# The preparation stage of a gated attention and S4 training kernel: parameter arithmetic on VectorE, gate sums as a row of a key projection, four staging tiles, later constant rows, value stores from GpSimd's queue

## Chip, cores and metric

The kernel runs on one core of a Trainium2 chip, as one launch. The metric is the device time of that launch in microseconds (us). The times given are medians over runs; the profile is of one execution.

## What is computed

The kernel computes the output of a gated mixture of two branches on the same input x (2048 positions, 576 features), and the gradients of everything but the second branch's own input. Cut to what matters:

```python
g = sigmoid((x * gate_w).sum(-1, keepdims=True))          # one gate per position
q, k, v = split_heads(x @ wqkv)                           # 32 heads of width 18
a = softmax(q @ k.T * 18**-0.5) @ v @ wo                  # branch A: attention

dt = exp(log_dt)[:, None]                                 # branch B: S4, 576 channels x 128 states
P  = exp(dt * (A_re + 1j*A_im) * l)                       # l = 0 .. 2047
K  = einsum("dn,dnl,dn->dl", C, P, dt * B).real
b  = causal_convolution(K, x) + x * Dskip
out = g * a + (1 - g) * b
# returned: out, and the gradients for x, wqkv, wo, A_re, A_im, B_re, B_im, C_re, C_im, log_dt, Dskip, gate_w
```

## The kernel before

The kernel has three stages that follow one another: preparation (lines 128 to 447), attention forward and backward in one loop (811 to 1263), then the S4 branch and the final products (1265 on). The change touches the preparation alone. In all three the order of instructions on each engine is the order in which the program issues them (a manual schedule, line 129): an engine that waits holds back all that is behind it on the same engine, and the DMA queue of SyncE (SP), which is written in the same way, does so too. Up to eight transfers issued from SP and ACT share a ring of eight completion semaphores, so a transfer also waits for the one that last used its semaphore.

Preparation, in the order of the program:

- Loads (182 to 198), all from SP: x in four blocks of four tiles of 128 positions, the K, Q and V columns of wqkv (`load_w`), gate_w broadcast to all partitions, the six S4 parameters (`load_prm`, three buffers `blk3` in turn), log_dt, then the constant rows of `QKV_d` (195 to 196, from a small DRAM tile `cst_d`) and wo.
- `x_turn` (213) transposes a block of x on TensorE into `xT`; `x_rev` (225) multiplies each tile by a reversal matrix, copies it to a staging tile `xr_t` (tag "xr", two buffers) and stores the staged block to DRAM (`xr_d`, line 234). Blocks 0 and 1 go ahead of the loop, 2 and 3 at its step 1.
- A loop of 30 steps (434 to 446). A step is one head group m (7 heads, the last 4), one of K, Q, V (`which` 1, 0, 2) and one half of the positions. It runs `proj` (347: ten matmuls of 512 columns into a PSUM tile of two buffers), `norms` of the step two before (363: two matmuls into one PSUM tile; for K a VectorE maximum `kmx`, for Q a ScalarE square root `qn`), `take` (384: the PSUM tile is copied to `stg`, by ScalarE, for the second half of V by VectorE, and squared on VectorE into `sq` for K and Q), and then the step's jobs. At the second half `stg` is stored to `QKV_d`: K and Q from ACT's queue, V from SP's (line 399; in the first group from SP as well).
- Jobs (409 to 426) are small pieces hung on steps: `prm_turn` (245, transposes of the parameters, steps 2 to 7), `gate_sum` (236: VectorE multiplies a tile of x by `gate_r` and sums each row, sixteen times, steps 0 to 10), `gate_fin` (239, step 11), `pars(k)` (297, steps 8 to 13: the S4 parameters, mostly on GpSimd through the helper `pl`, line 295; the results go to DRAM in `par_d`, `dt_d`, `prm_d` from GpSimd's queue), `wo_turn` (251, steps 12 to 16), `load_go` and `scale_go` (259 and 263: two loads of grad_out at step 7, and its products with g and 1 - g on VectorE at steps 14, 15, 20, 23, each of the first two followed by another load; the second product uses the tag "xr" too), and `da_turn` (274, steps 17 to 28).

Attention begins by loading strips of `QKV_d` from SP: `KaT_g` (line 854), `QaT_g` (865), and `Vtok_g` by a DMA transpose (869). Its tiles lie in memory that the preparation's pool has given back, so each waits for the last reader of what lay there. The first ScalarE work there is the exponential of line 1234. GpSimd begins with two memsets (841), loads `ez` from `par_d` (477) and then computes the S4 basis in the background (470, 523), and per block of queries `dOa` (908), which VectorE and TensorE wait for.

Of the kernel before, what the change touches and what calls it, by code (L numbers as in the profile page):

```python
# [20 lines left out]
def build(tc, aps, dbg_aps=None, stages=("s1", "attn", "post", "s4", "final")):  # L21
# [40 lines left out]
    with ExitStack() as gctx:  # L62
# [65 lines left out]
        with ExitStack() as ctx:  # L128
# [14 lines left out]

            xb = [s1.tile([P, TB, D], BF, name=f"xb{tb}") for tb in range(NBK)]
            blk3 = [s1.tile([P, DC, N], BF, name=f"pblk{q}") for q in range(3)]
            gate_r = s1.tile([P, D], BF, name="gate_r")
            gj = s1.tile([P, D], BF, name="gj")
            tmpb = s1.tile([P, D], BF, name="rowb")
            w_sb = s1.tile([P, DC, F], BF, name="wqkv_sb")
            xT = s1.tile([P, DC, S], BF, name="xT")  # L150
            wo_sb = s1.tile([P, DC, DPAD], BF, name="wo_sb")
            prm = s1.tile([P, 6, D], BF, name="prm")
            con = s1.tile([P, 3, S // P], BF, name="con")
            hsel = s1.tile([P, P], BF, name="hsel")
            gsum = s1.tile([P, NT], F32, name="gsum")
# [3 lines left out]
            for q_, v_ in enumerate((0.0, -1.0, 1.0)):  # L159
                GP.memset(con[:, q_, :], v_)  # L160
            GP.memset(hsel, 1.0)
# [7 lines left out]
            def load_w(which):  # L169
                sl = slice(which * D, (which + 1) * D)  # L170
                nc.sync.dma_start(w_sb[:, 0:nf, sl], wqkv[0:nf * P, sl].rearrange("(c p) n -> p c n", p=P))
                for y in range(2):
                    nc.sync.dma_start(w_sb[y * HB:(y + 1) * HB, nf, sl], wqkv[nf * P:D, sl])
# [7 lines left out]

            load_x(0, 0, 2)
# [6 lines left out]
            nc.sync.dma_start(gate_r, gate_w.rearrange("(o d) -> o d", o=1).to_broadcast([P, D]))  # L189
            load_prm(0)  # L190
            load_prm(1)
            load_w(2)
            nc.sync.dma_start(tmpb, log_dt.rearrange("(o d) -> o d", o=1).to_broadcast([P, D]))
            load_prm(2)
            for q_, (y0, y1) in enumerate(((DH + 1, HP), (DH, HS), (DH, HS))):
                nc.sync.dma_start(rows[q_][:, y0:y1, :], cst_d[q_:q_ + 1].unsqueeze(1).to_broadcast([H, y1 - y0, S]))
            nc.sync.dma_start(wo_sb[:, 0:nf, 0:D], wo[0:nf * P, :].rearrange("(c p) n -> p c n", p=P))
            nc.sync.dma_start(wo_sb[0:HB, nf, 0:D], wo[nf * P:D, :])
# [26 lines left out]
            def x_rev(t, eng):  # L225
                tb, q = divmod(t, TB)
                if q == 0:
                    xr_t[tb] = s1.tile([P, TB, D], BF, tag="xr", bufs=2, name="xr_t")
                ps = psJ.tile([P, 2, 512], F32, tag="pj", name="psr")
                for u in range(2):  # L230
                    mm(ps[:, u, 0:DH2], lhsT=J_bf, rhs=xb[tb][:, q, u * DH2:(u + 1) * DH2])
                copy_of(eng)(xr_t[tb][:, q, :].rearrange("p (u f) -> p u f", u=2), ps[:, :, 0:DH2])
                if q == TB - 1:
                    nc.sync.dma_start(xr_d[:, tb * TB:(tb + 1) * TB, :], xr_t[tb])

            def gate_sum(t):
                V.scalar_tensor_tensor(gj, xb[t // TB][:, t % TB, :], 1.0, gate_r, op0=A.mult, op1=A.mult, accum_out=gsum[:, t:t + 1])
# [7 lines left out]
            def prm_turn(r_, eng):  # L245
                b_ = blk3[r_ % 3]
                turn_rows([(b_[:, c, :], P, P) for c in range(nf)] + [(b_[0:HB, nf, :], HB, P)], None, eng, prm[:, r_, :])
# [9 lines left out]
            gob, dab = {}, {}  # L257

            def load_go(b):
                gob[b] = s1.tile([P, TB, D], BF, tag="go", bufs=2, name="go_b")  # L260
                nc.sync.dma_start(gob[b], go_v[:, b * TB:(b + 1) * TB, :])

            def scale_go(b):
                dab[b] = s1.tile([P, TB, D], BF, tag="d_a", bufs=2, name="d_a")
                gy_b = s1.tile([P, TB, D], BF, tag="xr", bufs=2, name="gy_b")
                for q in range(TB):
                    t = b * TB + q
                    V.tensor_scalar(dab[b][:, q, :], gob[b][:, q, :], g_t[:, t:t + 1], None, op0=A.mult)
                    V.tensor_scalar(gy_b[:, TB - 1 - q, :], gob[b][:, q, :], omg_t[:, t:t + 1], None, op0=A.mult)
                nc.sync.dma_start(gyr_d[:, NT - (b + 1) * TB:NT - b * TB, :], gy_b)  # L270
                if b + 2 < NBK:
                    load_go(b + 2)
# [12 lines left out]
            dt_b = s1.tile([P, D], F32, name="dt_b")  # L285
            adt = s1.tile([P, D], F32, name="adt")
            thn = s1.tile([P, D], F32, name="thn")
            t1 = s1.tile([P, D], F32, name="t1")
            Wn = s1.tile([P, 4, D], F32, name="Wn")
            wz = s1.tile([P, 2, D], F32, name="wz")  # L290
            zt = [s1.tile([P, 4, D], F32, name=f"zt{q}") for q in range(2)]
            POW = (1, P)

            def pl(o, a, b, op):
                GP.tensor_tensor(o, a, b, op=op)

            def pars(k):
                Ar_n, Ai_n, Br_n, Bi_n, Cr_n, Ci_n = [prm[:, r_, :] for r_ in range(6)]
                Wr, Wi = Wn[:, 0, :], Wn[:, 1, :]
                if k == 0:  # L300
                    AC.activation(dt_b, tmpb, ACT.Exp)
                    pl(adt, Ar_n, dt_b, A.mult)
                    pl(thn, Ai_n, dt_b, A.mult)
                elif k == 1:
                    for z_, p_ in zip(zt, POW):
                        AC.activation(z_[:, 0, :], adt, ACT.Exp, scale=float(p_))
                    for z_, p_ in zip(zt, POW):
                        V.tensor_scalar(z_[:, 2, :], thn, float(p_) * INV2PI, None, op0=A.mult)
                        V.tensor_scalar(z_[:, 1, :], z_[:, 2, :], MAGIC, -MAGIC, op0=A.add, op1=A.add)
                        V.tensor_tensor(z_[:, 2, :], z_[:, 2, :], z_[:, 1, :], op=A.subtract)  # L310
                elif k == 2:
                    pl(Wr, Cr_n, Br_n, A.mult); pl(t1, Ci_n, Bi_n, A.mult)
                    pl(Wr, Wr, t1, A.subtract); pl(Wr, Wr, dt_b, A.mult)
                    pl(Wi, Cr_n, Bi_n, A.mult); pl(t1, Ci_n, Br_n, A.mult)
                    pl(Wi, Wi, t1, A.add); pl(Wi, Wi, dt_b, A.mult)
                    GP.tensor_scalar(Wn[:, 2:4, :], Wn[:, 0:2, :], -1.0, None, op0=A.mult)
# [3 lines left out]
                elif k == 3:  # L320
                    for z_ in zt:
                        AC.activation(z_[:, 1, :], z_[:, 2, :], ACT.Sin, scale=0.5 * TWO_PI)
                        AC.activation(z_[:, 3, :], z_[:, 2, :], ACT.Sin, scale=0.25 * TWO_PI)
                else:
                    z_ = zt[k - 4]
                    gm, c_, s_, q_ = [z_[:, y, :] for y in range(4)]
                    pl(q_, q_, q_, A.mult)
                    GP.tensor_scalar(q_, q_, -4.0, 2.0, op0=A.mult, op1=A.add)
                    pl(s_, c_, q_, A.mult)
                    pl(c_, c_, c_, A.mult)  # L330
                    GP.tensor_scalar(c_, c_, -2.0, 1.0, op0=A.mult, op1=A.add)
                    pl(c_, gm, c_, A.mult)
                    pl(s_, gm, s_, A.mult)
                    if k == 4:
                        GP.dma_start(par_d[:, 8:10, :], z_[:, 1:3, :])
                        pl(wz[:, 0, :], Wr, c_, A.mult); pl(t1, Wi, s_, A.mult); pl(wz[:, 0, :], wz[:, 0, :], t1, A.subtract)
                        pl(wz[:, 1, :], Wr, s_, A.mult); pl(t1, Wi, c_, A.mult); pl(wz[:, 1, :], wz[:, 1, :], t1, A.add)
                        GP.dma_start(par_d[:, 4:6, :], wz)
                    else:
                        GP.tensor_scalar(q_, s_, -1.0, None, op0=A.mult)  # L340
                        GP.dma_start(par_d[:, 1:4, :], z_[:, 1:4, :])
                        GP.dma_start(par_d[:, 0:1, :], z_[:, 1:2, :])

            steps = [(m, which, pr) for m in range(len(hts)) for which in (1, 0, 2) for pr in range(2)]
            stgs, sqs = {}, {}

            def proj(s):
# [4 lines left out]
                w0 = which * D + h0 * DH  # L352
# [31 lines left out]
            def take(s, ps):  # L384
# [8 lines left out]
                on_v = which == 2 and pr == 1  # L393
                if which == 0:
# [3 lines left out]
                if pr == 1:  # L398
                    (nc.sync if on_v and s > 2 else AC).dma_start(rows[which][h0:h0 + hn, 0:DH, :], stg[0:fn, :])
# [9 lines left out]
            for r_, (s, e) in enumerate(((2, V), (3, V), (4, AC), (5, AC), (6, AC), (7, AC))):  # L409
                job(s, lambda r_=r_, e=e: prm_turn(r_, e))  # L410
            for k, s in enumerate((8, 9, 10, 11, 12, 13)):
                job(s, lambda k=k: pars(k))
            t = 0
# [1260 lines left out]
```

## Time and profile before

| what | us |
|---|---|
| median of 3 runs (2786.41 to 2802.28) | 2798.0 |
| profiled execution, its own time | 2800.34 |
| its span in the profile | 2798.6 |
| TensorE busy in the span | 2432.4 |
| VectorE busy | 2367.5 |
| ScalarE busy | 2367.9 |
| GpSimd busy | 1653.1 |
| first 160 us: TensorE / VectorE / ScalarE / GpSimd busy | 104.2 / 100.2 / 67.1 / 56.7 |
| first matmul of the attention stage starts at | 170.93 |

The profile is one execution; its span is 1.7 us shorter than the time of that execution, and that execution is 2.3 us above the median. Times in the views count from the start of the span. PE is TensorE, DVE VectorE, ACT ScalarE, POOL GpSimd, SP SyncE; "SPq" is SP's DMA queue issuing. L232 is line 232 of the kernel; a helper's line stands for all its callers.

### The profile page before, as it was taken

The page shows a single profiled execution, that of the slowest core. Times are in us where ns is not written, and L with a number is a line of the kernel's source. Part 1 is how long each engine was busy: PE and PEld are TensorE (multiplying, and loading weights), DVE is VectorE, ACT ScalarE, POOL GpSimd, SP SyncE. Part 2 cuts the span into 40 slices and gives each one's busy share as a digit, 9 for nine tenths or more (in the row PEclk, how much of TensorE's full clock was granted, in tenths as well). Part 3 has the DMA queues.
Part 4 walks back from the last instruction along what each step waited for, and adds up shares of the span by engine and source line. Part 5 has one row for each costly group of instructions (what it writes and reads, how often), then busy time and mean ns, then how long its engine had stood idle before and what let it go on. Part 6 is the DMA issues. An engine that isn't in the chain of part 4 may idle for free.

```text
span 2798.6 us, 70648 instructions
## 1 busy us (share of the span) xinstructions
PE 2432.4 (87%) x27379; PEld 1166.5 (42%) x27379; DVE 2367.5 (85%) x4862; ACT 2367.9 (85%) x2749; POOL 1653.1 (59%) x2694
## 2 busy tenths in 40 slices
PE   6678989989898889989989998898885899988789
PEld 3332333333233333333333333333323888888557
DVE  4837999999888999989999999898885899999944
ACT  3459999999999999999999999999974788888221
POOL 0757887988888798888878879878701000000010
PEclk8888999999998999999999999999987898899899
DMA  6435889879988988998897898798669998986996
GB/s 201 158 93 129 158 157 181 159 163 170 164 157 148 181 165 158 176 172 151 165 177 157 160 180 156 160 167 166 153 131 214 243 248 215 246 239 173 252 238 136
DMA packets 1253515, 490.95 MB, mean 175 GB/s; under 512 B 1150005, under 2 KB 1224486, under 8 KB 1243962
## 3 DMA queue, kind: packets, MB, share of 16 engines
q1 hardware_dynamic: 1218282, 416.29, 72.8%
q0 software_dynamic: 21536, 57.40, 8.0%
q10 hardware_dynamic: 13360, 12.75, 1.6%
q8 instruction: 214, 3.51, 0.5%
q14 instruction: 123, 1.01, 0.1%
HBM read 145.83 MB, written 98.52 MB: 87 GB/s over the span
## 4 chain that ended last, share of the span: by engine, by line
ACT 36%; PE 24%; DVE 24%; issue 6%; DMA 5%; POOL 3%; SPq 1%; ACTq 0%; DVEq 0%; POOLq 0%
ACT eb L1239 21%; ACT PT L1234 13%; PE ps_P L30 7%; DVE ds L1244 7%; DVE tz L672 3%; PE accV L30 2%; DVE tz L674 2%; PE turn_p L956 2%; DVE HG L676 2%; PE ps_dx L30 2%; PE ps_proj L30 2%; DVE pq L742 1%; PE accK L30 1%; POOL et L470 1%; DVE dvacc L1010 1%
## 5 line engine op out<-in xcount | busy, mean ns | idle before, releaser
L1244 DVE TENSOR_TENSOR ds<-ps_P,PT 128x512 bf16<-128x512 f32 x2048 | 1310.9, 682 | 136.5 <-PE ps_P L30 89.5
L1239 ACT ACTIVATE eb<-ps_P 128x1024 bf16<-128x1024 f32 x1024 | 1099.9, 1074 | 39.9 <-PE ps_P L30 39.9
L1234 ACT ACTIVATE PT<-ps_P 128x1024 bf16<-128x1024 f32 x1024 | 1105.2, 1080 | 24.0 <-PE ps_P L30 22.5
L30 PE MATMUL ps_P<-dOaT,VaT_g 32*128 32x512 bf16 x2048 | 579.9, 391 | 30.0 <-DVE ds L1244 15.4
L470 POOL TENSOR_TENSOR et<-eG,eT 128x448 f32<-128x448 f32 x576 | 542.2, 961 | 10.7
L30 PE MATMUL ps_P<-QaT_g,KaT_g 32*128 32x512 bf16 x2048 | 405.7, 388 | 140.1 <-ACT PT L1234 122.7
L30 PE MATMUL ps_P<-KaT_g,QaT_g 32*128 32x512 bf16 x2048 | 409.5, 392 | 2.0 <-ACT eb L1239 1.5
L30 PEld LDWEIGHTS <-KaT_g 32*128 32x128 bf16 x2048 | 147.9, 91 | 467.2 <-issue 451.4
L470 POOL TENSOR_TENSOR Eo<-et,et 128x448 bf16<-128x448 f32 x288 | 326.9, 1135 | 20.8
L778 POOL TENSOR_TENSOR SS<-m 128x96 f32<-128x96 f32 x18 | 9.5, 528 | 428.7 <-ACT m L776 428.7
L30 PEld LDWEIGHTS <-QaT_g 32*128 32x128 bf16 x2048 | 116.2, 91 | 289.7 <-issue 267.5
L30 PE MATMUL accV<-eb,dOa 128*32 128x512 bf16 x2048 | 186.7, 398 | 27.6 <-ACT eb L1239 27.2
L30 PE MATMUL accO<-PT,Vtok_g 128*32 128x512 bf16 x2048 | 208.4, 396 | 0.1
L30 PE MATMUL accK<-dsT,Qtok_g 128*32 128x256 bf16 x4096 | 163.9, 281 | 15.9 <-DMA dsT<-ds 14.1
L30 PE MATMUL accQ<-ds,Ktok_g 128*32 128x512 bf16 x2048 | 162.5, 396 | 2.1 <-DVE dvacc L1010 2.0
L30 PEld LDWEIGHTS <-Vtok_g 128*32 128x32 bf16 x2048 | 52.8, 93 | 221.8 <-issue 221.8
L961 DVE COPY dsT<-turn_p 128x1024 bf16<-128x1024 bf16 (+1 forms) x216 | 138.8, 643 | 1.8 <-PE turn_p L956 1.7
L956 PE MATMUL turn_p<-ident_bf,ds 128*128 128x128 bf16 x1664 | 134.9, 224 | 2.1 <-DVE dkacc L1047 0.9
L633 ACT COPY E1e<-etp 128x1024 bf16<-128x1024 bf16 x136 | 128.9, 1063 | 4.3 <-PE etp L632 4.1
L672 DVE TENSOR_TENSOR tz<-HG,par 128x128 f32<-128x128 f32 x504 | 123.4, 284 | 0.6
L470 POOL TENSOR_TENSOR et<-eT 128x32 f32<-128x32 f32 (+3 forms) x288 | 115.8, 422 | 11.4
L30 PEld LDWEIGHTS <-Qtok_g 128*32 128x32 bf16 x4096 | 88.3, 97 | 80.4 <-issue 54.6
(257 smaller groups left out, 3737.7 us busy)
## 6 DMA issues: line engine op xcount, KB each, us to landing
E_d<-Eo POOLq DMA_DIRECT2D x144, 256.0 KB, 3.4
E1n<-E_d SPq DMA_DIRECT2D x36, 1024.0 KB
xs<-xb_d SPq DMA_DIRECT2D x18, 1024.0 KB
T0w<-Kp_d SPq DMA_DIRECT2D x18, 1024.0 KB
Md_d<-mst SPq DMA_DIRECT2D x36, 288.0 KB
dsT<-ds SPq DMA_TRANSPOSE x512
dqkv_d<-dtk POOLq DMA_DIRECT2D x96, 72.0 KB, 4.1
skw<-Md_d SPq DMA_DIRECT2D x72, 64.0 KB
```

The source lines that it names most:

```text
L30: return nc.tensor.matmul(out, lhsT=lhsT, rhs=rhs, start=start, stop=stop, **kw)
L470: nc.gpsimd.tensor_tensor(out, a, b, op=op)
L633: copy(E_[:, 4 * q:4 * q + 4], pt_)
L672: nc.vector.tensor_tensor(tz[s_], HG[:, s_, :, k - 1, :].unsqueeze(1).to_broadcast([P, 2, 2, CB]), ZZ, op=A.mult)
L674: nc.vector.tensor_tensor(tz[s_][:, 0], tz[s_][:, 0], UVk[:, :, s_, k, :], op=A.add)
L676: nc.vector.tensor_tensor(HG[:, s_, :, k, :], tz[s_][:, 0], tz[s_][:, 1, ::-1], op=A.add)
L742: nc.vector.tensor_tensor(o.rearrange("p a b n c -> p a b (n c)"), a_.rearrange("p b n c -> p b (n c)").unsqueeze(1).to_broadcast([P, 2, 2 ...
L956: nc.tensor.transpose(pt_[:, x, qb, :], t_[:, qb * P:(qb + 1) * P], ident_bf)
L961: (nc.scalar.copy if NTOT <= now[0] < NTOT + OFF else nc.vector.tensor_copy)(o_(), pt_[:, x:x + n])
L1234: nc.scalar.activation(U["PT"][i, j // 2], ps, ACT.Exp)
L1239: nc.scalar.activation(e, ps, ACT.Exp)
L1244: nc.vector.tensor_tensor(U["ds"][i][:, j, :], ps, U["PT"][i, j // 2][:, j % 2, :], op=A.mult)
```

## The change

All of it is in the preparation.

- Parameters: `pars` has eleven pieces instead of six, at steps 6, 7, 8, 9, 10, 11, 12, 16, 17, 22, 23. All arithmetic is on VectorE (`tt`) with both powers side by side in one operand of 1152 elements; exponentials and sines stay on ScalarE. GpSimd keeps the stores.
- Gate sums: gate_w is loaded as one more column of the weights, 24 zero columns behind the K columns (`GCOL`), so that the K projection of the last head group gives the sums as row 96 of its PSUM tile. ScalarE copies that row (`gate_take`), eight one-column matmuls turn it into columns (`gate_turn`). The last head group therefore runs second: m in the order 0, 4, 1, 2, 3. The sixteen `gate_sum` operations go.
- Staging: tag "xr" has four buffers. `d_a` takes these tiles afterwards; grad_out is loaded over the tiles of x, all four blocks at step 3, and its second product is written in place and stored tile by tile (16 stores in place of 4). `scale_go` comes in halves at steps 13 to 16 and 18 to 21.
- Loads: the gate column follows wq; parameters, log_dt and wv are issued after step 0 and so behind the first two `xr_d` stores; wo at step 2, constant rows at step 4. The turns of the last two parameters move to steps 8 and 9.
- V stores go out from GpSimd's queue.
- The order of allocation changes, so that the tiles of attention lie over other tiles of the preparation (`zt` is now the first).

```diff
+            WOFF = {1: 0, 0: 608, 2: 1184}
+            GCOL, GROW = D + 24, 96
+            zt = s1.tile([P, 4, 2, D], F32, name="zt")
+            w_sb = s1.tile([P, DC, 1760], BF, name="wqkv_sb")
...
+            V.memset(w_sb[:, :, D:GCOL], 0.0)
+            V.memset(one_f, 1.0)
...
+            def load_gate():
+                nc.sync.dma_start(w_sb[:, 0:nf, GCOL], gate_w[0:nf * P].rearrange("(c p) -> p c", p=P))
+                for y in range(2):
+                    nc.sync.dma_start(w_sb[y * HB:(y + 1) * HB, nf, GCOL:GCOL + 1], gate_w[nf * P:D].rearrange("(p o) -> p o", o=1))
...
-                    xr_t[tb] = s1.tile([P, TB, D], BF, tag="xr", bufs=2, name="xr_t")
+                    xr_t[tb] = s1.tile([P, TB, D], BF, tag="xr", bufs=4, name="xr_t")
...
-            def gate_sum(t):
-                V.scalar_tensor_tensor(gj, xb[t // TB][:, t % TB, :], 1.0, gate_r, op0=A.mult, op1=A.mult, accum_out=gsum[:, t:t + 1])
+            def gate_take(pr, ps):
+                zrow[pr] = s1.tile([P, 2 * TW], F32, tag="zrow", name="zrow")
+                AC.copy(zrow[pr][GROW:GROW + 1], ps[GROW:GROW + 1].rearrange("p a b -> p (a b)"))
+
+            def gate_turn(pr):
+                z_ = zrow.pop(pr)
+                pz = psT.tile([P, 512], F32, tag="tr", name="pz")
+                nb = 2 * TB
+                for q in range(nb):
+                    mm(pz[:, q:q + 1], lhsT=z_[GROW:GROW + 1, q * P:(q + 1) * P], rhs=one_f[GROW:GROW + 1, :], tile_position=(GROW, 0))
+                V.tensor_copy(gsum[:, pr * nb:(pr + 1) * nb], pz[:, 0:nb])
...
+                for q in range(q0, q0 + 2):
                     t = b * TB + q
-                    V.tensor_scalar(dab[b][:, q, :], gob[b][:, q, :], g_t[:, t:t + 1], None, op0=A.mult)
-                    V.tensor_scalar(gy_b[:, TB - 1 - q, :], gob[b][:, q, :], omg_t[:, t:t + 1], None, op0=A.mult)
-                nc.sync.dma_start(gyr_d[:, NT - (b + 1) * TB:NT - b * TB, :], gy_b)
+                    V.tensor_scalar(dab[b][:, q, :], xb[b][:, q, :], g_t[:, t:t + 1], None, op0=A.mult)
+                    V.tensor_scalar(xb[b][:, q, :], xb[b][:, q, :], omg_t[:, t:t + 1], None, op0=A.mult)
+                    nc.sync.dma_start(gyr_d[:, NT - 1 - t, :], xb[b][:, q, :])
...
+                elif k == 4:
+                    tt(Wn[:, 2:4, :], prm[:, 4:6, :], prm[:, 2:4, :], A.mult)
+                    tt(tp, prm[:, 4:6, :], prm[:, 3:1:-1, :], A.mult)
+                    tt(Wn[:, 0, :], Wn[:, 2, :], Wn[:, 3, :], A.subtract)
+                elif k == 5:
+                    tt(Wn[:, 1, :], tp[:, 0, :], tp[:, 1, :], A.add)
+                    tt(Wn[:, 0:2, :], Wn[:, 0:2, :], bc, A.mult)
+                    V.tensor_scalar(Wn[:, 2:4, :], Wn[:, 0:2, :], -1.0, None, op0=A.mult)
+                    GP.dma_start(par_d[:, 6:8, :], Wn[:, 2:4, :])
...
-            steps = [(m, which, pr) for m in range(len(hts)) for which in (1, 0, 2) for pr in range(2)]
+            steps = [(m, which, pr) for m in (0, 4, 1, 2, 3) for which in (1, 0, 2) for pr in range(2)]
+            GATE = (4, 1)
...
-                    (nc.sync if on_v and s > 2 else AC).dma_start(rows[which][h0:h0 + hn, 0:DH, :], stg[0:fn, :])
+                    (GP if on_v else AC).dma_start(rows[which][h0:h0 + hn, 0:DH, :], stg[0:fn, :])
...
-            for r_, (s, e) in enumerate(((2, V), (3, V), (4, AC), (5, AC), (6, AC), (7, AC))):
+            for r_, (s, e) in enumerate(((2, V), (3, V), (4, AC), (5, AC), (8, AC), (9, AC))):
...
-            for k, s in enumerate((8, 9, 10, 11, 12, 13)):
+            for k, s in enumerate((6, 7, 8, 9, 10, 11, 12, 16, 17, 22, 23)):
...
-            job(11, gate_fin)
-            job(7, lambda: [load_go(b) for b in range(2)])
+            job(12, gate_fin)
+            job(2, load_wo)
+            job(3, lambda: [load_go(b) for b in range(NBK)])
+            job(4, load_const)
...
+                if s == 0:
+                    late_tiles()
+                    load_prm(0)
+                    load_prm(1)
+                    nc.sync.dma_start(prm_t["tmpb"], log_dt.rearrange("(o d) -> o d", o=1).to_broadcast([P, D]))
+                    load_w(2)
+                    load_prm(2)
```

## Prediction

> **What bounds the kernel now.** I read the page first, then busy time by stretches of 10 us, then the waits, then the chain in order of time, all for the preparation.
>
> ```profile
> PE   6678989989898889989989998898885899988789
> DVE  4837999999888999989999999898885899999944
> ACT  3459999999999999999999999999974788888221
> ```
>
> Each digit is 70 us. The first two are low on all three engines, then ScalarE stands at 9 for most of the attention. What the preparation saves should therefore come off the end one for one: attention starts earlier and does not run faster. By stretches (us, then per engine busy time and count, granted clock, DMA):
>
> ```profile
> 20.00:30.00 10.00, 0.00 (x0) 0.00 (x0) 0.00 (x0) 0.00 (x0) 0.00 (x0) 0.61 0.96 234
> ...
> 80.00:90.00 10.00, 0.00 (x0) 0.00 (x0) 9.86 (x11) 2.58 (x4) 9.44 (x6) 0.51 0.00 0
> ...
> 100.00:110.00 10.00, 3.64 (x20) 1.88 (x20) 10.00 (x9) 1.02 (x1) 9.37 (x8) 0.87 0.44 148
> ...
> 160.00:170.00 10.00, 0.00 (x0) 0.00 (x0) 0.00 (x0) 0.00 (x0) 8.83 (x29) 0.50 0.74 112
> ```
>
> Four holes of TensorE: one with only DMA, two under VectorE and GpSimd busy together, one at the border to attention. The waits of the first 180 us name them (total, times, longest):
>
> ```profile
> PE psr L30 <- ACT xr_t L232: 19.5, 2, 18.8
> ACT xr_t L232 <- DMA xr_d<-xr_t: 19.1, 1, 19.1
> ...
> PE ps_P L30 <- DMA QaT_g<-QKV_d: 15.1, 1, 15.1
> ...
> PE ps_proj L30 <- DVE stg L397: 13.6, 2, 13.1
> ...
> PE ps L30 <- DVE kmx L373: 9.9, 2, 9.6
> ```
>
> The first hole is the third staging tile waiting for the first one's store, which SP issued only at 23.91 us, behind the constants and wo, and which landed at 36.5. The next two are PSUM tiles that VectorE frees late. Why VectorE is late shows by form of operation (count, busy, mean ns), first in the preparation, then late in the kernel where GpSimd is nearly idle:
>
> ```profile
> L310 DVE TENSOR_TENSOR zt<-zt 128x576 f32<-128x576 f32 x2 | 3.5, 1772 | 0.1
> ...
> L268 DVE TENSOR_SCALAR d_a<-go_b,g_t 128x576 bf16<-128x576 bf16 x16 | 13.6, 849 | 0.0
> ```
>
> ```profile
> L1393 DVE TENSOR_TENSOR fta<-zz,SS 128x576 f32<-128x576 f32 x6 | 4.5, 748 | 0.0
> ...
> L1497 DVE TENSOR_SCALAR Wri_f<-Wri_f 128x576 f32<-128x576 f32 x1 | 0.5, 453 | 0.0
> ```
>
> The same subtraction shape takes 1772 ns beside GpSimd and 748 without it; `d_a` takes 0.35 us where GpSimd rests and 1.5 where it works. The border, from the chain:
>
> ```profile
> 155.87 1.11 ACT qn L380
> 157.35 0.59 SPq L854
> ...
> 162.76 2.34 SPq L869
> 165.22 5.58 DMA QaT_g<-QKV_d
> ```
>
> The strips for attention are issued only after the last V store, since both are in SP's queue.
>
> [...] Here GpSimd's stores of 288 to 864 KB landed 3.1 to 8.4 us after issue. [...] The trace has the 1.28 (at 66.76), and the exponential follows at 68.06[...].
>
> **The change part by part.** Landmarks before: step 1 starts on TensorE at 43.3, step 6 at 58.0, the last `qn` at 155.9, the first exponential of attention at 171.6.
>
> *Four tiles, loads moved behind the stores.* Reversals of blocks 2 and 3 no longer wait for any store. Last work before the hole ends at 18.4, the wait ends at 36.5: 18.1 us go. The remaining reversal, 37.2 to 43.3, ran at half clock (0.50) and becomes about 5: in all -18.5 (17 to 20). Is something else late then? Step 1 needs wk, long there; wq for step 2 was complete by 16.5; wv, now behind the gate column and two stores, is needed at step 4, near 33, and its 0.65 MB should land by 26 at 250 GB/s. The gate column is 640 elements of 2 bytes; nothing to 5 us, taken 2, hidden, because SP's next items (`xr_d`, parameters, wv) have slack of that size.
>
> *Steps 1 to 5.* 14.7 us, bound by TensorE (2.7 to 3.1 a step, by what turns and norms stand in it). Unchanged.
>
> *Steps 6 to 29.* Before 97.9 us. I walked these steps with trace durations: projection 2.2, norms 0.45, a turn 0.5 to 0.65; ScalarE copy 1.0, `qn` 1.1; VectorE `sq` 0.67, `kmx` 1.21, V copy 1.22, scaling 0.36 each.
> - Parameters on VectorE: 12 two-operand operations of 1152 at 1.35 (between 748 for 576 and L691's 2159 for 1920), 4 of 576 at 0.75, single-operand ones at 0.75 and 0.45: 23 us. Off VectorE go gate sums (16.9 + 1.3), the old L308 to L310 (9.5), and the excess of scaling (24.7 to 11.5) and `sq` (3): 44. GpSimd is left with stores.
> - Gate: ScalarE row copies 2 x 1.0 (an operation of 1024 columns costs that whatever its rows), 16 one-column matmuls. None is shown; nearest are L898's float32 transposes, 0.165 each. I take 0.15, 2.4 us in all; bounds 0.1 to 0.3.
> - A new wait: the row tile has one buffer, and step 7's row copy stands on ScalarE ahead of step 7's `stg` copy while step 8's `gate_turn` still has to read the old row. So ScalarE waits through projection 8, norms, a turn and eight matmuls, about 2.5 us beyond its own work; projection 9 waits for the `stg` copy queued behind it, and `kmx`, `sq` and the sines follow late. Cost in the walk: 4 us.
> - Sums by six steps: steps 6 to 11 TensorE 18.1, VectorE 17.5, ScalarE 19.0, with the new wait 24; steps 12 to 17 TensorE 17.6, VectorE 22, now the bound; 18 to 23 TensorE 18.3, VectorE 19.3; 24 to 29 17.5, as measured (138.35 to 155.87). The walk overlaps neighbours and ends at 81.5.
> So -16.5 (10 to 21).
>
> *V stores and strips at the border.* SP now reaches the strips after its last `gyr_d` store (step 21); `KaT` waits for the last reader of `zt` (step 22), `QaT` for the semaphore of the K store of step 25. With some 3 us for that store and the 5.6 that `QaT` took, it lands about 3 us before the last step ends. Left are `qn` 1.1, table load 1.28, half a microsecond: 3 in place of 15.7, -12.7 (-14 to -8). Behind it the first five rounds ran 8.3 us at clock 0.54 where later ones take 6.3; a warm TensorE saves 0 to 2, taken 1. Of the V stores on GpSimd, each buffer is reused five steps, 15 us, later: covered by landing times up to 8.4. GpSimd starts its own work after the last V store, only some 36 us earlier against 49 for the rest; before its first `dOa` it had idled 21.5 us, so this is covered too, with about 8 to spare.
>
> *Small slips* (a parameter turn waiting for a late load, 16 small stores): +2.7.
>
> Sum: 18.5 + 16.5 + 12.7 + 1 - 2.7 = 46. Against the profiled execution, 2800.3 - 46 = 2754; the median is 2.3 lower, so 2752.
>
> **Rivals.**
> A. *A late follower at the border.* GpSimd's `dOa` or `QaT` comes late and half of the border gain stays a wait. For it: the thin margins just named. Against: POOL's 21.5 us. Gain about 36: 2762.
> B. *VectorE is slow by itself.* If 1.4 to 1.8 us were the true price of float32 here, parameters cost 23 more on the engine that then bounds: gain 23, 2775. Against it stands 748 ns.
> C. *The queue moves its hole.* Loads, 2.4 MB of grad_out and 2.2 MB of constants pushed together at steps 3 and 4 (some 18 us at 250 GB/s) delay C_im, and with it step 9, by 8 to 12 us: 2763. It needs those transfers ahead of the parameter loads on all engines; C_re is ahead of them, C_im is not.
> D. *The stages are not additive or the change does not take effect*, gain under 14: 2791.
> E. *Slower: the clock.* TensorE loses its pauses before attention. In the stretch 700 to 880 us the clock was 0.94 and ScalarE busy 171.8 of 180, in its neighbours 1.00 and 180: 8 us lost. If a denser start brought this to more than six of the ten stretches, the gain would be used up; at eight, 2816. Nothing shows such a memory over 180 us.
>
> **How the numbers follow.** Forecast 0.64, A 0.13, B 0.07, C 0.10, D 0.03, E 0.03. The forecast's own bounds (parts at both ends, not all at once, plus a scatter of 8 us in the runs before) give 2737 to 2766; A and C widen that to 2772, leaving B, D, E out. A measurement of this kernel can tell about 0.5%, 14 us, from no change. Faster by more: 0.94; within: 0.03; slower: 0.03.
>
> **What would show it.** Right: no wait of `xr_t` for `xr_d`; step 1 near 25 us; VectorE tensor operations of 1152 at 1.3 to 1.4; ScalarE idle 2 us or more ahead of the second row copy; first exponential of attention near 124; the rest shifted alike. Wrong: TensorE waiting for `pblk` or wv (C), VectorE at double price (B), `QaT` or `dOa` in the waits near 125 to 175 (A), clock under 1.00 in mid-attention (E).

## The result and the profile after

The changed kernel takes 2756.4 us (median of 4 runs, 2746.4 to 2761.0) against 2795.1 beside it, a ratio of 0.9858 (95% interval 0.9818 to 0.9898). Run once more among the experiments it took 2758.5 (0.9855, 0.9833 to 0.9878). The profiled execution took 2755.7, its span is 2754.0.

The forecast, 2752, was close. Its sum was not made of what it said, and most of this section and the next is about that. The page of the changed kernel, the slices of TensorE, VectorE and ScalarE:

```profile
PE   8798989988989988889999889988885899999789
DVE  5649999999999998899999989998985899999954
ACT  5489999999999999999999999999974788888221
```

Before, TensorE's and ScalarE's first two digits were 6 6 and 3 4; they are 8 7 and 5 4 now, and from the fourth digit on the rows look as they did. By stretches of 10 us in the changed kernel (us, then busy time and count of TensorE, its weight loads, VectorE, ScalarE, GpSimd, then clock, DMA share, GB/s):

```profile
20.00:30.00 10.00, 8.34 (x57) 4.91 (x55) 4.68 (x7) 4.85 (x6) 0.00 (x0) 1.00 0.78 236
...
50.00:60.00 10.00, 9.80 (x43) 4.91 (x42) 8.41 (x13) 7.97 (x11) 0.00 (x0) 0.67 0.64 218
...
80.00:90.00 10.00, 8.41 (x53) 4.62 (x51) 9.83 (x18) 6.72 (x9) 2.10 (x3) 1.00 0.47 141
...
100.00:110.00 10.00, 9.98 (x60) 5.50 (x58) 8.57 (x14) 5.58 (x9) 1.22 (x2) 1.00 0.60 186
...
120.00:130.00 10.00, 0.28 (x2) 0.00 (x0) 1.14 (x2) 2.39 (x2) 3.25 (x11) 0.69 0.88 151
```

Three of the four holes are filled. The fourth, at the border to attention, has only moved from 160 to 120 us. A new weak spot shows at 50 to 60: TensorE counts as busy for 9.80 us, but at a mean clock of 0.67, with 43 matmuls where the stretch from 100 us on has 60. The waits of the first 200 us name both (total, times, longest):

```profile
PE ps_P L30 <- DMA QaT_g<-QKV_d: 12.5, 1, 12.5
...
ACT zrow L259 <- PE pz L30: 3.2, 1, 3.2
...
PE ps_proj L30 <- ACT stg L422: 2.2, 1, 2.2
```

Landmarks, read off the timelines (start times in us):

| | before | changed | change of the stretch | forecast |
|---|---|---|---|---|
| step 1 of the loop | 43.32 | 23.93 | -19.4 | -18.5 |
| step 6 | 57.99 | 38.60 | 0.0 | 0 |
| last `qn` | 155.87 | 120.31 | -16.2 | -16.5 and +2.7 of slips |
| first exponential of attention | 171.58 | 133.43 | -2.6 | -12.7 |
| 51st exponential | 244.72 | 206.50 | -0.1 | -1 |
| end of the span | 2798.6 | 2754.0 | -6.4 | 0 |

Preparation and border give 38.2 us, which is nearly the difference of the medians (38.7). The last 6.4 are the profiled execution's own. In a second profile of the changed kernel (e10) the stretch from first exponential to end took 2626.1 us, against 2627.0 before and 2620.6 in the first profile. In the profiles of both kernels TensorE waits 1.4 to 2.5 us now and then inside attention (for the transfer `dsT` or ahead of the transpose `turn_p`), at different places, and within 2 us of the end of such a wait half clock (0.50 in the clock records) begins, for 3.4 to 17.1 us (before: from 756.0, 875.5 and 1192.9 us; changed: from 1141.0 and 1898.8). This scatter is in every comparison of single profiles below, so experiments are read at the landmarks first. The landmarks scatter too: in the changed kernel and its variants step 6 starts between 38.5 us (e12) and 40.4 us (e4), and where the code of the border is the same, the way from last `qn` to first exponential took 11.2 us (e1) to 14.6 us (e10), 13.1 in the profile above.

### The profile page after: what moved, and what is told of

Its sections match the earlier page's. It is cut to its first block, busy times and chain, and to the rows that moved or that the text cites. A ratio compares the mean times of both kernels' runs of the same rounds, so it can differ in the third digit from the quotient of the medians.

```text
span 2754.0 us, 70696 instructions
## 1 busy us (share of the span) xinstructions
PE 2429.9 (88%) x27411; PEld 1170.9 (43%) x27411; DVE 2348.6 (85%) x4850; ACT 2368.6 (86%) x2749; POOL 1611.9 (59%) x2667
## 3 DMA queue, kind: packets, MB, share of 16 engines
q10 hardware_dynamic: 13360, 12.75, 1.6%
## 4 chain that ended last, share of the span: by engine, by line
ACT 38%; PE 26%; DVE 23%; issue 6%; DMA 4%; POOL 2%; SPq 1%; ACTq 0%; DVEq 0%; POOLq 0%
ACT eb L1271 22%; ACT PT L1266 14%; DVE ds L1276 7%; PE ps_P L30 7%; DVE tz L704 3%; PE accV L30 2%; PE ps_dx L30 2%; PE turn_p L988 2%; DVE tz L706 2%; DVE HG L708 2%; PE accK L30 1%; PE ps_dwq L30 1%; DVE pq L774 1%; PE misc L30 1%; DMA dsT<-ds 1%
```

## Where the border's gain went

The chain of work of the changed kernel, followed through the border (start, duration, what):

```profile
100.29 9.06 DMA gyr_d<-xb
...
109.43 0.70 SPq L886
...
110.19 3.73 SPq L886
...
113.97 1.67 SPq L886
...
115.69 7.54 SPq L886
...
123.27 4.31 SPq L901
...
127.64 5.01 DMA QaT_g<-QKV_d
```

SP does reach the strips early, at 109.4, as forecast. Then it takes 18 us to issue four `KaT` strips and one `Vtok`, which took 7.7 us before the change. `QaT` stands behind them, is issued at 127.64 and lands 12 us after the start of the last `qn`.

The completion marks of a transfer, that is, the updates of its semaphore that the trace records, give its landing time. The K store of step 25, whose semaphore `QaT` needs (the next transfer on a semaphore is issued once the one before has landed: in this kernel at 14.50 us after a landing at 14.43), was issued at 108.62 and landed 15.2 us later, at 123.8 (the forecast had taken "some 3 us"); so the store alone would have held `QaT` until then, and the strips ahead of it in SP's queue held it 3.8 us longer. The four `KaT` strips landed 16.0 to 18.6 us after issue, 7.3 to 8.4 before the change. Even in the kernel before, the stores from ScalarE's queue had taken 5.4 to 10.9 us; this was to be read there, and was not.

The marks have a pattern. A store of seven heads from ScalarE's or SP's queue shows 8 marks, one of four heads 5, a `KaT` strip of four heads 5, but a `QaT` strip or a `gyr_d` store 16; a V store from GpSimd's queue shows 16, with the same access as a K store. Heads of K lie 20 rows apart; heads of Q lie 32 rows apart, and a strip of four is one run of 128 rows. From SP's and ScalarE's queues the marks are thus the number of heads and one more, 7 + 1 and 4 + 1, and 16 for the run. From GpSimd's queue they are 16 with seven heads too, while the number of packets in flight is the same: a K store of seven heads has seven packets in flight for about two thirds of its time, both from ScalarE's queue (changed kernel, issued at 27.26) and from GpSimd's (e4, issued at 29.36).

What can differ is which engines carry it. No record here gives an engine's number, but the number of packets in flight speaks for the sharing. From 112 to 122 us two stores from ScalarE's queue, up to four `KaT` strips and the rest of GpSimd's stores were under way, and all together had seven packets in flight for 62% of the time and seven or fewer for 88%. The stretch itself, with the columns from above:

```profile
112.00:122.00 10.00, 8.28 (x45) 3.96 (x43) 5.89 (x13) 4.30 (x5) 0.35 (x1) 1.00 0.39 113
```

A DMA share of 0.39 is 6.2 of 16 engines. So the DMA as a whole was not short. That the K and Q stores and the K strips queued for the same seven engines or so, while the others stood idle, is an inference from these counts.

## The experiments

All runs but e8 start from the changed kernel; `A` stands for its store line in the edits:

```
A: (GP if on_v else AC).dma_start(rows[which][h0:h0 + hn, 0:DH, :], stg[0:fn, :])
```

Two theories stood against each other on the border. The forecast's: V stores in SP's queue hold the strips back, and moving them is enough. The other: the K and Q stores from ScalarE's queue crowd the few DMA engines that the strips need.

**e4: K and Q stores from GpSimd's queue too.**

```diff
-A: (GP if on_v else AC).dma_start(...)
+A: GP.dma_start(...)
```

> The changed kernel with the K and Q stores issued from GpSimd's queue as the V stores are, instead of from ScalarE's queue. Theory (a store from ScalarE's queue is spread over few DMA engines, 8 completion marks against 16, and lands 12 to 15 us after its issue late in the preparation; that keeps the strips back): stores land in 5 to 10 us, the KaT strips land within 9 us of their issue, first exponential at 122 to 126 instead of 133.4; ScalarE is rid of ten issues of 0.7 us. Time 7 to 12 us lower. Rival ([...]stores from there land later still when there are three times as many): landings over 12 us, and the border stays or grows; time the same or up to 5 us higher.

SP's issues in e4 (start, duration, what, count):

```profile
103.86 2.50 SPq L886 DMA_DIRECT2D KaT_g<-QKV_d  x4
106.47 1.98 SPq L901 DMA_TRANSPOSE Vtok_g<-QKV_d  x1
108.56 2.66 SPq L897 DMA_DIRECT2D QaT_g<-QKV_d  x1
```

What took 18 us takes 4.6. The `KaT` strips land 3.9 to 7.3 us after issue, `QaT` at 119.7, before the last `qn` (120.63). First exponential at 123.43: 2.8 us of border, the forecast's 3. ScalarE is also rid of its ten issues, but that is not the gain: the last `qn` comes no earlier than before (120.31). The stretch in which the strips move:

```profile
104.00:114.00 10.00, 9.95 (x60) 5.30 (x58) 7.37 (x12) 4.92 (x8) 1.79 (x3) 1.00 0.77 185
```

Twice the DMA share, 12.3 engines: two stores from GpSimd's queue reach 14 packets in flight together (116 to 119 us), two from ScalarE's queue in the changed kernel never more than eight (116 to 123 us). So the expectation was right about the crowding and wrong about its cause: a store has no more packets in flight from GpSimd's queue, but two together have nearly twice as many. That successive stores no longer pile up on the same engines is an inference from this. The stores land in 5.5 to 11.9 us, beyond the 10 of the theory but not over 12, and the border shrinks, so the rival (landings over 12 us) is refuted as an account of the border. Whether a store still waits in part for GpSimd is open: its first mark comes 1.6 to 8.5 us after the issue. Time 2752.1, 0.983 (0.9806 to 0.9854): by itself too close to the changed kernel to tell; e11, which adds a second row buffer, is clear of it.

**e3: the first Q strip ahead of three K strips.**

```diff
                             piece(m)
+                            if m == 0:
+                                load_piece("QaT", 0, 0)
+                                load_piece("Vtok", 0, 0)
...
```

(and the two are skipped where they were issued before.)

> The changed kernel with the first QaT strip and the first Vtok strip issued on SP right behind the first KaT strip, ahead of the three other KaT strips. Theory (QaT waits on SP behind strips that are not needed yet): QaT lands before 123, the wait at the border is then ended by the first KaT strip, which landed at 126.6: first exponential at 127 to 128 instead of 133.4, time 5 to 6 us lower. Rival (the strips are late because the DMA engines they use are full of stores): whatever the order, the last of the needed strips lands at 131 to 133 and the time stays within 2 us.

SP's issues in e3:

```profile
109.81 0.70 SPq L886 DMA_DIRECT2D KaT_g<-QKV_d  x1
110.56 1.98 SPq L900 DMA_DIRECT2D QaT_g<-QKV_d  x1
112.60 5.76 SPq L904 DMA_TRANSPOSE Vtok_g<-QKV_d  x1
118.41 9.80 SPq L886 DMA_DIRECT2D KaT_g<-QKV_d  x3
```

`QaT` is issued 17 us earlier and lands at 129.5, 18.9 us after its issue (5.0 in the changed kernel). First exponential at 130.25, last `qn` at 121.69: 8.6 us of border. Against borders of 11.2 to 14.6 us in the old order, the order is worth 3 to 6 us; the crowding is what remains. Both expectations missed in part. Time 2751.2, 0.9836 (0.9809 to 0.9864).

**e7: V stores back on SP. e12: V stores back on SP, K and Q stores on GpSimd's queue.**

```diff
-A: (GP if on_v else AC).dma_start(...)
+A: (nc.sync if on_v and s > 2 else AC).dma_start(...)     # e7
+A: (nc.sync if on_v and s > 2 else GP).dma_start(...)     # e12
```

> The changed kernel with the V stores back on SP's queue. Prediction's account (V stores in SP's queue are what holds the strips back, 12.7 us): 10 us or more slower. Present account (from GpSimd's queue the strips are issued earlier but crawl behind stores, so that the move gained only about 2.6 us at the border): strips issued after the last V store at 121 to 122, first exponential at 134 to 138, time 1 to 5 us higher.

> The changed kernel with K and Q stores from GpSimd's queue and the V stores back on SP's. Theory (moving the V stores is worth the 12 us that the prediction gave it as soon as the strips are not slowed by the K and Q stores): strips are issued only after the last V store at 121 to 122, first exponential at 133 to 137 instead of 123.4. Rival (the K and Q stores were all that mattered): first exponential at 124 to 128.

SP's issues in e12:

```profile
105.16 16.55 SPq L424 DMA_DIRECT2D QKV_d<-stg  x2
121.91 5.23 SPq L886 DMA_DIRECT2D KaT_g<-QKV_d  x4
127.18 3.80 SPq L901 DMA_TRANSPOSE Vtok_g<-QKV_d  x1
131.03 0.58 SPq L897 DMA_DIRECT2D QaT_g<-QKV_d  x1
```

In e12 the strips wait behind the last V store: first exponential at 136.62, border 16.5 us, where e4 has 123.43 and 2.8. So moving the V stores is worth 13 us when K and Q stores are out of the way. In e7 it is at 136.96, border 16.2, against 11.2 to 14.6 with the changed kernel's border: there the same move is worth 2 to 5. And with the V stores on SP, moving K and Q gains nothing (16.5 against 16.2). It takes both moves. Times: e12 2758.0 (0.9858, 0.9835 to 0.9882); e7 2770.7 (0.9903, 0.9875 to 0.9931). The e7 median lies higher than its landmark explains: its profiled execution took 2763.9, the three others 2769.8 to 2779.9. By its times e7 fits the first of its expectations, by its landmark the second; what slowed the other three is open.

**e1: two staging tiles again. e8: the kernel before with later constant rows and wo alone.**

```diff
-xr_t[tb] = s1.tile([P, TB, D], BF, tag="xr", bufs=4, name="xr_t")
+xr_t[tb] = xr_t[tb - 2] if tb > 1 else s1.tile([P, TB, D], BF, tag="xr", bufs=4, name="xr_t")   # e1
```

```diff
 # e8, on the kernel before: the lines of the constant rows and of wo as load_const() and load_wo()
+            job(2, load_wo)
+            job(4, load_const)
```

> The changed kernel with the staging tiles of blocks 2 and 3 being those of blocks 0 and 1 again, as before the change; the load order stays the changed one. Theory of the prediction (the four tiles end the wait): the third tile waits for the first xr_d store again, step 1 starts at 27 us or later instead of 23.93, and the time grows by 3 to 8 us. Rival (the later constant rows and wo end it by themselves): that store is issued at 12.65 and has landed at 18.05, before the third tile is wanted; step 1 starts within 0.7 us of 23.93 and the time stays within 3 us.

> The kernel before with one part of the change alone: the issues of wo and of the constant rows moved into the loop, to steps 2 and 4; two staging tiles, all else as before. Theory (the load order ends the first hole by itself): step 1 starts at 24 to 27 us instead of 43.3, time 16 to 19 us below that of before. Rival (the parameter loads and wv still stand ahead of the first store of a staging tile): step 1 at 28 to 33, time 9 to 14 us lower. Rival (the gain is given back at steps 13 to 16, where VectorE and GpSimd bound): less than 6 us lower.

In e1 step 1 starts at 24.01 (23.93 with four tiles): the first store is issued at 12.75 and has landed at 18.16, and the third tile is first written at 18.29, so it just fits. The time is 2758.0 (0.9861, 0.9844 to 0.9878), as the changed kernel's. With the later loads the four tiles buy nothing. In e8 the first store leaves at 18.55 in place of 23.91 and lands at 23.8 in place of 36.4. ScalarE's wait for it, 19.1 us before, is in e8:

```profile
ACT xr_t L235 <- DMA xr_d<-xr_t: 6.1, 1, 6.1
```

Step 1 starts at 31.12, 12.2 us earlier; the other 7.2 of the 19.4 belong to the parameter loads and wv, which the full change also puts behind the stores, or there to the tiles. The first exponential comes 9.4 us earlier, 2.8 being lost on the way, and the time is 2790.0, 0.9968 (0.9956 to 0.998): the second of the three expectations.

**e9: the parameters' arithmetic on GpSimd.**

```diff
             def tt(o, a, b, op):
-                V.tensor_tensor(o, a, b, op=op)
+                GP.tensor_tensor(o, a, b, op=op)
```

(and the single-operand ones of `pars` from its sixth piece on likewise; a fused pair becomes two.)

> The changed kernel with the parameters' two-operand arithmetic back on GpSimd at the same steps and in the same 1152-element pieces (two of the fused VectorE operations become two each). Theory of the prediction (GpSimd work slows VectorE beside it, and is slower itself): VectorE's scalings of grad_out take 0.6 to 1.5 us instead of 0.36 where GpSimd works, sq more than 0.68, and the last qn comes 6 to 16 us later than 120.3; time 6 to 16 us higher. Rival (VectorE, rid of some 20 us of work in the stretch in which it bounds, gets faster, GpSimd working beside it for nothing): the last qn comes 1 to 4 us earlier.

The last `qn` comes at 147.90, 27.6 us later, 26.0 of it in steps 6 to 29: more than the expectation's upper end, and more than all that these steps had gained. Why is in two timelines of e9. VectorE:

```profile
76.76 0.36 DVE L297 TENSOR_SCALAR d_a<-xb,g_t 128x576 bf16<-128x576 bf16 x1
77.16 0.37 DVE L298 TENSOR_SCALAR xb<-xb,omg_t 128x576 bf16<-128x576 bf16 x1
77.44 3.04 DVE L297 TENSOR_SCALAR d_a<-xb,g_t 128x576 bf16<-128x576 bf16 x1
80.52 3.19 DVE L298 TENSOR_SCALAR xb<-xb,omg_t 128x576 bf16<-128x576 bf16 x1
...
87.46 3.14 DVE L298 TENSOR_SCALAR xb<-xb,omg_t 128x576 bf16<-128x576 bf16 x1
```

and GpSimd:

```profile
78.19 2.12 POOL L313 TENSOR_TENSOR zt<-zt 128x1152 f32<-128x1152 f32 x1
80.41 3.13 POOL L345 TENSOR_SCALAR zt<-zt 128x1152 f32<-128x1152 f32 x1
...
87.30 3.13 POOL L348 TENSOR_SCALAR zt<-zt 128x1152 f32<-128x1152 f32 x1
```

Three scalings, of 0.36 to 0.37 us where they stand alone, meet a GpSimd operation (one of 2.12 us, two of 3.13); they take 3.04 to 3.19 us and end 0.17 us after it. All scalings and `sq` together take 50.1 us of VectorE in e9, 22.5 in the changed kernel. TensorE waits 21.1 us for `kmx` in the same run. The border is only 3.7 us there, since the strips have all the time they need; first exponential 18.1 us later than in the changed kernel. The time is 2767.0, 0.9898 (0.987 to 0.9925), 8.5 above the changed kernel on the same chip; the profiled execution won 10 us back after its first exponential, and by which mechanism is open.

**e2: two buffers for the gate row. e5: the row turned by transfers.**

```diff
-zrow[pr] = s1.tile([P, 2 * TW], F32, tag="zrow", name="zrow")
+zrow[pr] = s1.tile([P, 2 * TW], F32, tag="zrow", bufs=2, name="zrow")      # e2, e5
...
+GP.dma_start(gz_d[pr:pr + 1, :], z_[GROW:GROW + 1, :])                     # e5, for the matmuls
+GP.dma_start(gsum[:, pr * nb:(pr + 1) * nb], gz_d[pr].rearrange("(q p) -> p q", p=P))
```

> The changed kernel with two buffers for the gate row (zrow). Theory: the single buffer costs the 3.2 us wait of ScalarE at 45 to 48 us, the TensorE pause of 2.2 us behind it, and the half clock that the trace shows from 48.7 on, under which step 9 took 7.4 us. Without it steps 6 to 11 take 19 to 21 us instead of 25.9, the last qn comes 5 to 7 us earlier (114 to 115), and the time falls by 3 to 7 us, less what the border keeps. Rival 1 (only the bare wait counts): 2 to 3 us earlier. Rival 2 (the border is set by transfers that do not start earlier): the last qn comes earlier, the first exponential of attention stays at 133.

> The changed kernel with two buffers for the gate row, and the row turned into columns by two transfers through DRAM (GpSimd's queue) in place of 16 one-column matmuls. With two buffers alone the clock still halved twice for 3.4 us, each time within 1.2 us after a group of one-column matmuls, and step 6 to the last qn took 78.6 us (81.7 in the changed kernel). Theory (the one-column matmuls, 2 x 1.94 us, count for the clock as pauses): clock 1.00 through steps 6 to 11, step 6 to last qn 71 to 74 us, last qn at 110 to 113. Rival (ScalarE, busy 20.6 of 25.9 us there, or the load of C_im bounds these steps): 76 to 78 us.

The stretch 38.6 to 64.46, which is steps 6 to 11 of the changed kernel (the other two enter step 6 at 40.2 and 40.1), with the columns of the stretches above. The changed kernel:

```profile
38.60:64.46 25.86, 23.69 (x111) 12.15 (x111) 13.40 (x19) 18.50 (x20) 0.69 (x1) 0.80 0.69 234
```

e2, with two rows:

```profile
38.60:64.46 25.86, 25.86 (x129) 13.27 (x127) 15.82 (x20) 20.58 (x23) 0.71 (x2) 0.87 0.72 244
```

e5, with transfers in place of the matmuls:

```profile
38.60:64.46 25.86, 20.95 (x97) 9.60 (x95) 17.57 (x20) 20.51 (x23) 4.22 (x6) 0.93 0.78 244
```

With two rows the wait goes and steps 6 to 11 take 22.7 us in place of 25.9; step 6 to last `qn` 78.6 in place of 81.7. The clock still drops, and the timeline of e2 shows around what:

```profile
47.67 1.94 PE L30 MATMUL pz<-one_f,zrow 1*128 1x1 f32 x16
...
49.54 3.49 PE L30 MATMUL ps_proj<-xT,wqkv_sb 128*72 128x512 bf16 x10
```

Half clock begins at 50.3 and again at 57.1, each time within 1.2 us after such a group, though TensorE never stops (busy 25.86 of 25.86 us; the same in e11, at 48.7 and 55.5); a projection of 2.2 us takes 3.2 to 3.5. Why it begins after 1.94 us of one-column matmuls was not shown.

In e5, without them, steps 8 to 10 run at full clock (2.22 to 2.25 us a projection), and yet step 6 to last `qn` takes 78.0 us: ScalarE, busy 20.5 of 25.9 us with table loads (1.28 us each), exponentials and sines, lets TensorE wait 2.6 us at step 11, and half clock follows there (the next projection takes 3.32 us). The rival was right. The first exponential comes at 130.86 and 130.36 (borders 12.1 and 12.2), 2.6 and 3.1 us earlier; the border scatters by more than that, so these two runs do not tell how much of a saving it keeps. Times 2753.5 (0.9843, 0.9812 to 0.9874) and 2752.1 (0.9836, 0.9813 to 0.9859).

**e6 and e11: savings together.** e6 is e5 with e4's stores, e11 is e4's stores with two rows.

> The run before, and K and Q stores from GpSimd's queue as well (as in e4_all_stores_pool, whose first exponential came at 123.4). Theory (the two savings add): first exponential at 115 to 118, time 2742 to 2747. Rival (the strips for attention become late again, since they stand on SP behind the gyr_d stores, which hang on the gates): first exponential at 119 to 122, time about 2748 to 2751.

> The changed kernel with K and Q stores from GpSimd's queue and two buffers for the gate row. Each alone brought the first exponential to 123.4 and to 130.9 in place of 133.4. Theory (they add, since the first takes away the wait for strips and the second time of the steps): first exponential at 120 to 122, time 10 to 13 us below the changed kernel on the same chip. Rival (what is saved ahead of attention is partly lost within it, as in the two runs that had 10 us less there and gained 4): 3 to 6 us below.

e6: last `qn` at 119.94, first exponential at 122.73, later than either expectation; `gate_fin` waits 2.7 us for the transfer of the gate column, which shares GpSimd's queue with the K stores. TensorE also waits 2.6 us for the load of C_im, the wait of the prediction's rival C, and runs at half clock for 6.8 us from then on. Time 2751.6 (0.9837, 0.9818 to 0.9857): nothing more than e4. e11: last `qn` 117.13, first exponential 119.92, so the two savings add, and the time is 2746.2, 0.9808 (0.9784 to 0.9831), 12.3 us below the changed kernel beside it. It is the best version tried: at the first exponential it is ahead of e4 by 3.5 us and of e2 by 10.9; by time its interval overlaps with theirs.

**e10: the changed kernel again.**

> The changed kernel once more, unchanged, beside the others on the same chip: first exponential at 133 to 134 as in the first profile, time 0.983 to 0.988 of before.

First exponential at 136.80, last `qn` at 122.18: the border is 14.6 us in this execution, a gain of 1.1 on the kernel before, where the first profile has 2.6 and e1 4.5. The ratio is as expected, the landmark 3 us later than expected.

## Why the prediction was right, and where it was wrong

**First hole, -18.5: right (-19.4), for half of the named reason.** The step named four tiles and later loads together. e1 shows that the tiles do nothing once the loads are later; e8 that constants and wo are 12.2 of it. Whether four tiles alone would have done it was not tried. wv had landed at 26.2 us, 26 forecast from 250 GB/s (251 in the first 30 us before the change). The 2 us for the gate column were an estimate that no record before bears out: its three transfers landed 5.6 to 6.4 us after issue, as `gate_r` had before (6.1).

**Steps 1 to 5, unchanged: right** (14.67 us both times).

**Steps 6 to 29, -16.5: right (-16.2).** By six steps 25.9, 18.3, 19.7 and 17.9 us were measured, 24, 22, 19.3 and 17.5 forecast. The price of VectorE's operations holds, by form in the changed kernel:

```profile
L298 DVE TENSOR_SCALAR xb<-xb,omg_t 128x576 bf16<-128x576 bf16 x16 | 5.9, 370 | 0.6
L297 DVE TENSOR_SCALAR d_a<-xb,g_t 128x576 bf16<-128x576 bf16 x16 | 5.8, 362 | 0.0
...
L313 DVE TENSOR_TENSOR zt<-zt 128x1152 f32<-128x1152 f32 x3 | 4.0, 1346 | 0.0
```

1346 ns for 1152 elements (1.35 us forecast), and the two scalings at 0.36 and 0.37. That is the end of rival B. A row copy on ScalarE takes 1.00 us for its one row (1.00 for 72 and for 126 rows before). The new wait for the row tile is there (3.2 us), and cost 3.1 by e2 (4 forecast). Two terms were mis-sized and cancelled: the one-column matmuls took 3.9 us, not 2.4 (16 records per group of eight), and half clock followed each group (6.8 us from 48.7, behind a pause of 2.2 us as well, and 3.4 us from 59.0); steps 12 to 17, where VectorE was to bind at 22, took 18.3. The slips of 2.7 did not show apart. The forecast counted 16 us of VectorE's time as the excess of scalings and `sq` beside GpSimd; in e9, with the parameters on GpSimd, these operations take 28 us more. Its 26.0 us at the last `qn` hold GpSimd's own longer operations as well; the two were not separated.

**Border, -12.7: wrong (-2.6; -1.1 in e10, -4.5 in e1).** The step that failed is "With some 3 us for that store and the 5.6 that `QaT` took, it lands about 3 us before the last step ends". The store took 15.2 us, the strips ahead of `QaT` took SP 18 us to issue, and `QaT` landed 12 us after the last step. The mechanism of the step, V stores in SP's queue, was right: with the crowding gone it is worth 13 us (e12 against e4). It was not enough, since the strips, issued early, ran into the K and Q stores that had been over by then before. Rival A named this place and "`QaT` comes late". Its words and its sum disagree: half of the border's gain would leave a gain of about 40, but its 36 takes off 10, four fifths. The loss in the first profile was 10.1.

**Warm TensorE, -1: did not come** (-0.1). The term rested on the border's wait going; it stayed, and the clock was again at one half for 17 us about the start of attention (from 123.8 on).

**The total** came out close by luck. In the profiled execution (2755.7, forecast 2754) the border's missing 10 us were made up by a first hole 0.9 larger, slips of 2.7 that were not needed, and 6.4 us of scatter. By the medians 38.7 us were gained of 46 forecast, 7 short; the result is only 4.4 from 2752 because the kernel before took 2795.1 beside it, not the 2798.0 that the forecast set out from. C and E did not occur: C_im's late load shows in no wait of the first profile (it landed at 52.1 and was wanted at 55.1, in a step that was itself late; e6, without that delay, waited for it), and attention from first to last exponential took 1872 to 1883 us in all fourteen profiles, whenever it began.

## What to carry to other kernels

Before counting on a transfer that is to move ahead, read its landing time in the company that it will have, not alone (15.2 us for a store put at 3): count the packets that it has in flight, and list what else is under way then. A low DMA share while transfers crawl was the sign here (0.39, with seven packets in flight or fewer for 88% of the time). A load order can do the work of extra buffers; try it first. When work moves to or from GpSimd, price the VectorE operations beside it by the length of the GpSimd operation that they may meet (0.37 us became 3.19 beside one of 3.13), not by a mean.

## What the hardware showed that was not expected

- Issuing a 128 KB strip from SP took 0.5 to 0.7 us (e4) or up to 7.54 us (changed kernel), with no semaphore left to wait for in the last case: the marks of the transfer that it waits for were complete at 110.8, and the issue ended at 123.2. What held it back is not shown.
- The same K store shows 8 marks from ScalarE's queue and 16 from GpSimd's, and seven packets in flight from both. From 112 to 122 us the DMA share was 0.39 (6.2 of 16 engines) while `KaT` strips took 16 us and more.
- A strip of Q, with 16 marks, landed 5.0 us after issue once the stores were through (changed kernel), and 18.9 us after issue among them (e3).
- A VectorE operation of 128x16 elements took 3.10 us beside GpSimd's 3.44 us operation in e9 (0.20 us in the changed kernel).
- 1.94 us of one-column matmuls without a pause (e2, e11), or a pause of 2.6 us without them (e5, e6), were followed by 3.4 to 6.8 us of half clock.
